# A recurrent attention and a maxout network on one core: another order of all engines' work

## The chip, the core and the metric

The kernel runs on one core of a Trainium2 chip. The core has TensorE (PE), VectorE (DVE), ScalarE (ACT), GpSimd (POOL) and a queue, SyncE (SP), from which the kernel issues nearly all of its DMAs. The metric is device microseconds of one execution. The kernel before takes 147.53 us, the median of 3 runs (147.34 to 148.29).

## The reference

Two parts, one behind the other. The first is a recurrent attention with a decay for each row of its state, over 4 batches, 8 heads, 768 tokens and a head size of 48:

```python
for t in range(S):
    state = alpha[:, :, t, :, None] * state + np.einsum('bhd,bhe->bhde', k[:, :, t], v[:, :, t])
    y[:, :, t] = np.einsum('bhd,bhde->bhe', q[:, :, t], state)
```

The heads of a token are then put side by side, which gives x with 3072 rows of 384, and a feed-forward network with three gates follows (w1, w2, w3 are 384x768, w_out is 768x384):

```python
h = np.maximum(np.maximum(x @ w1, x @ w2), x @ w3)
return h @ w_out
```

All inputs and the output are float32; the kernel works in float16 with sums in float32.

## The kernel before

The 3072 tokens are cut into 12 **steps** of 256 tokens: step s is chunk s // 4 of batch s % 4. A step has two units (x = 0 and 1) of 128 tokens, and the state of a batch goes from unit to unit. What is done for a step is cut into **pieces**, each a small function that issues one or a few instructions. Nothing plans their order: it is a text, `ORDER` (line 507), of 824 pieces such as `G6@1`, and `emit` (line 501) calls them one after the other. The letter names the piece, the number is its index, the number behind @ the step, and a letter between them chooses the engine where there is a choice: v for DVE, a for ACT, p for GpSimd. Each engine works strictly in the order in which its own pieces stand in that text, and waits where an operand, or a buffer that it is to write, is not ready.

The pieces, by the line that shows in the profile:

- **l, K** load an input (l0 alpha, l1 k, l2 q, l3 v; line 100) or a part of a weight (K0 to K8 of the gates, line 111; K9 to K11 of w_out, line 114), 384 KB each, from SP's queue. Inputs go into rings of 4 buffers, weights into 8 staging buffers. **W** casts a weight part to float16 (GpSimd if no letter is given).
- **H** (line 489) is a warm-up matmul on zeroed data; its result is not used. There are 35.
- **m, N, r, u, w** prepare the decays: m multiplies pairs of alphas (line 192), N and r are logs and inverses on ACT (lines 197 to 208), u and w multiply k and q by them (lines 212 and 216). **c** sums the logs with PE into a PSUM bank `lps`; **f, e, g** are exponentials of it on ACT (lines 244 and 255).
- **k, q** scale k and q by the exponentials (line 261, products of two 128x384 SBUF tiles into `qk`). **V** scales v into `vt`, **v** copies it by units into `vu`.
- **T** transposes `qk` with PE into `tps`, and **t** copies that to `qkT` (128x1024); from step 5 on **D** does both as a DMA transpose from SP's queue (line 304).
- **A** (line 318) computes scores into two banks `aps`, each for half of the heads; **a** (line 327) multiplies each of four banks of a step by the causal mask, always on DVE, into `lat`.
- **S** (line 411) sums k times v into `sps`; **s** adds the kept state to it, **M** and **z** multiply by the decay, **y** casts the result into `st` for the next unit.
- **Y** (line 341) computes y from the scores (Y0, Y2) and from the state (Y1, Y3) into `yps`; **x** casts it to `xT`.
- **G** (line 442) is one of nine gate products of a step: `Gi` with i = 3 jg + g is gate g for a third jg of the 768 columns; six 128x256 matmuls into a bank `gps`. It needs the weight part of the same number. **h** takes it out of PSUM: a cast where g = 0 (on ACT unless a letter says otherwise), a maximum with the one before on DVE where g is 1 or 2 (line 459). **O** (line 475) multiplies by w_out, and **o** scales the result (line 164 or 166) and issues the store (line 484).

All PSUM tiles share one ring of 8 banks (`bank`, line 181), handed out in the order of the text, so a PE piece can wait for an `h`, `a`, `s` or `t` that has yet to read an old bank. SP has at most 8 of its DMAs under way: each waits for the one eight places earlier, and a DMA that waits for its data holds all behind it.

```python
for piece in order.split():
    piece, _, step = piece.partition("@")
    i = piece[1:].rstrip("vpa")
    pieces[piece[0]](int(step), int(i), piece[1 + len(i):])
```

Of the kernel before, what the change touches and what calls it, by code (L numbers as in the profile page):

```python
# [25 lines left out]
def kernel(  # L26
# [474 lines left out]
    def emit(order):  # L501
# [16 lines left out]
        G3@0 G3@1 Y0@2 Y3@2 h3a@1 W5p@0 h4v@1 s1v@2 m0v@4 G5@1 x0a@2 h3a@0 G5@0 x1a@2 N0@4 k1v@3 G1@2 G0@2
        G3@2 c0@4 G4@2 h5v@1 h4v@0 w0p@3 K8@0 q1p@3 h0a@2 h3a@2 T1@3 G5@2 u0p@3 h5v@0 h4v@2 q0p@3 k0p@3
        T0@3 W6a@0 f0@4 e0@4 t0a@3 g0@4 V0p@3 t1v@3 h1v@2 h5v@2 m0v@5 G6@1 G6@0 A0@3 A1@3 S0@3 h6a@1 r0@4  # L520
        s0a@3 N0@5 M1p@0 W7p@0 a3@3 h6v@0 a1@3 G2@2 G6@2 G7@1 G7@0 z0p@3 a0@3 h2v@2 a2@3 c0@5 y0a@3 W8a@0
        G8@2 G8@0 l2@4 K10@0 u0p@4 k0p@4 z1p@0 q1p@4 k1p@4 h7v@0 s1v@3 h8v@0 r1@4 y1a@0 l3@4 Y3@3 Y0@3
        x0v@3 G8@1 h7v@1 h8v@1 G7@2 h6a@2 W10a@0 w0p@4 x1a@3 V0a@4 T1@4 G3@3 K11@0 q0p@4 T0@4 e0@5 t1a@4
        h7v@2 h8v@2 l1@5 t0v@4 G7@3 G0@3 u0p@5 K9@0 f0@5 h3a@3 g0@5 h0a@3 l0@6 l3@5 v0p@4 A0@4 l2@5 l0@7
        S0@4 A1@4 W9a@0 W11a@0 k0v@5 M0v@5 a1@4 m0v@6 l0@8 l1@6 l2@6 s0v@4 N0@6 v1a@4 r0@5 M0v@4 M1p@1
        z1p@1 z0p@4 V0p@5 k1p@5 q1p@5 a0@4 a3@4 G1@3 G6@3 G5@3 l3@6 O1@2 h1v@3 a2@4 o1v@2 s1v@4 c0@6 m0p@7
        f0@6 h6a@3 O0@2 G2@3 h7v@3 h2v@3 g0@6 e0@6 r1@5 y0a@4 G4@3 S0@5 Y1@4 Y2@4 Y3@4 Y0@4 O0@1 D1@5 r0@6
        x1a@4 x0a@4 N0@7 r1@6 r0@8 w0v@5 q0p@5 h4v@3 h5v@3 s0v@5 q1p@6 u0p@6 D0@5 G0@4 l1@7 l2@7 z0v@5
        G3@4 c0@7 w0p@6 q0p@6 s1v@5 h0v@4 k1v@6 o0v@2 k0p@6 y1p@1 h3v@4 G4@4 O0@0 G8@3 G1@4 D0@6 D1@6
        h8v@3 h1v@4 G7@4 O1@1 f0@7 v1a@5 l1@8 l0@9 h4v@4 l2@8 r1@8 e0@7 r0@7 g0@7 l3@7 V0a@6 o0a@1 v0v@5  # L530
        A0@5 A1@5 a1@5 a3@5 M1p@3 m0p@8 o0a@0 N0@8 a2@5 a0@5 M0v@6 O1@0 G6@4 c0@8 h6a@4 G2@4 g0@8 o1a@0
        y0p@5 u0v@7 r1@7 h2v@4 o1v@1 M1p@2 z1p@2 v1p@6 k1p@7 Y1@5 Y0@5 w0p@7 x0v@5 q0p@7 Y3@5 Y2@5 h7v@4
        e0@8 x1a@5 f0@8 G8@4 G5@4 G6@5 v0p@6 h5v@4 M0p@8 q1p@7 G7@5 G3@5 h8v@4 h6a@5 S0@6 A1@6 A0@6 h7v@5
        k0v@7 s0v@6 a3@6 a0@6 a1@6 D1@7 D0@7 l0@10 l1@9 l2@9 O0@4 z0p@6 a2@6 M0p@7 y1p@2 y0v@6 s1v@6 M1v@4
        O1@4 G8@5 G0@5 Y3@6 Y1@6 Y0@6 x0v@6 o0v@4 h8v@5 Y2@6 x1v@6 u0v@8 h3a@5 z1p@4 k1p@8 m0p@9 k0p@8
        w0p@8 q0p@8 h0a@5 G1@5 O0@3 G4@5 G2@5 G5@5 D0@8 q1v@8 h4v@5 D1@8 l3@8 N0@9 V0a@7 h1v@5 h5v@5 G3@6
        G4@6 v1a@7 h3a@6 h2v@5 h4v@6 G6@6 o0a@3 h6a@6 A0@7 A1@7 S0@7 a2@7 v0p@7 z1p@3 a1@7 o1v@4 s0v@7
        r0@9 r1@9 O1@5 z0p@7 u0p@9 G0@6 G2@6 c0@9 a0@7 h0a@6 l2@10 l3@9 l0@11 s1v@7 m0v@10 a3@7 G5@6 G1@6
        G7@6 O0@5 r0@10 y1a@3 h1v@6 h5v@6 y0v@7 h7v@6 O1@3 l1@10 G8@6 e0@9 o0a@5 r1@10 o1a@3 f0@9 g0@9
        Y1@7 Y0@7 w0p@9 h2v@6 V0v@8 x0a@7 Y3@7 Y2@7 x1a@7 N0@10 A0@8 S0@8 A1@8 G6@7 s0v@8 c0@10 f0@10  # L540
        h8v@6 a3@8 q0p@9 M1p@5 z1p@5 k0p@9 v0p@8 y1p@4 D0@9 h6a@7 a0@8 a2@8 G8@7 o1a@5 k1v@9 q1v@9 z0v@8
        G1@7 G3@7 v1p@8 D1@9 h3a@7 y1a@5 V0a@9 y0a@8 G4@7 h4v@7 a1@8 G0@7 O1@6 m0p@11 G5@7 Y0@8 Y2@8 Y1@8
        Y3@8 h0v@7 h5v@7 h1v@7 x0v@8 N0@11 g0@10 o1a@6 x1a@8 G7@7 c0@11 e0@10 f0@11 w0p@10 u0p@10 M1p@6
        G2@7 G0@8 G3@8 h7v@7 h8v@7 h2v@7 M0v@9 G1@8 e0@11 r0@11 g0@11 O0@7 A1@9 v0a@9 h0a@8 h3v@8 k1v@10
        S0@9 A0@9 h1v@8 M1v@7 z1v@6 k0p@10 q0p@10 q1p@10 s0v@9 r1@11 l2@11 G4@8 G6@8 a2@9 z0p@9 w0v@11
        a1@9 G7@8 O1@7 G5@8 M0p@10 q1p@11 M0p@11 l3@10 l1@11 y0p@9 D1@10 D0@10 V0p@10 v1a@9 y1a@6 h6a@8
        G8@8 h7v@8 a0@9 a3@9 h8v@8 O0@6 o1a@7 o0a@7 G2@8 h4v@8 o0v@6 k1p@11 h2v@8 h5v@8 Y3@9 Y1@9 Y0@9
        Y2@9 x0a@9 x1a@9 A1@10 A0@10 S0@10 a3@10 D1@11 l3@11 V0a@11 a2@10 a1@10 G4@9 G6@9 u0p@11 q0p@11
        G3@9 G1@9 G5@9 k0v@11 s0v@10 h3v@9 h4v@9 G8@9 G7@9 h5v@9 D0@11 O1@8 h6v@9 a0@10 h7v@9 G0@9 v0p@10
        z0p@10 y0p@10 v1p@10 h8v@9 Y0@10 Y1@10 x0v@10 Y3@10 Y2@10 z1p@7 y1v@7 h0a@9 x1a@10 S0@11 A0@11  # L550
        A1@11 s0v@11 o1v@8 a0@11 z0v@11 a1@11 a3@11 h1v@9 a2@11 v1p@11 y0p@11 v0a@11 G2@9 O0@8 G3@10 G0@10
        G7@10 G4@10 h2v@9 Y3@11 Y0@11 Y2@11 Y1@11 h3v@10 h0a@10 x0a@11 h4v@10 x1v@11 G5@10 G6@10 G1@10
# [40 lines left out]
```

## Time and profile before

| | us |
|---|---|
| median of 3 runs | 147.53 |
| the profiled execution | 146.9 |
| its span | 145.1 |
| 648 matmuls of the gates (line 442), busy | 77.9 |
| 150 matmuls of the output projection (line 475), busy | 26.6 |
| 35 warm-up matmuls (line 489), busy | 11.7 |
| 48 masks on DVE (line 327), busy | 30.7 |
| 72 maxima on DVE (line 459), busy | 48.6 |

The page gives one profiled execution. The granted TensorE clock is 1.0 throughout. DMA moves 250 to 350 GB/s up to about 53 us, and little after 120 us. Busy time alone does not tell what bounds the kernel: the chain of waits and the timeline do, and the prediction shows their lines.

### The profile page before, as it was taken

How to read it: one execution, taken by the hardware profiler on the slowest of the kernel's cores; microseconds unless marked ns; L12 is line 12 of the kernel's file. 1: busy time of each engine (PE TensorE's matmuls, PEld its weight loads, DVE VectorE, ACT ScalarE, POOL GpSimd, SP SyncE). 2: the span in 40 equal slices, each digit the busy share in tenths (PEclk: the TensorE clock that was granted, in tenths of full speed). 3: DMA queues.
4: the chain of work that ended last, by engine and by line, in shares of the span. 5: the costliest groups of instructions: out<-in, count | busy, mean ns of one | idle time of the engine just before them, and what ended most of it. 6: DMA issues, size and time to landing. Idle time of an engine off the chain costs nothing.

```text
span 145.1 us, 5795 instructions
## 1 busy us (share of the span) xinstructions
PE 138.5 (95%) x2450; PEld 107.0 (74%) x2450; DVE 124.6 (86%) x238; ACT 86.0 (59%) x178; POOL 94.4 (65%) x139
## 2 busy tenths in 40 slices
...
GB/s 118 321 325 325 354 249 339 299 268 300 273 335 332 271 290 299 156 220 208 290 330 171 249 204 250 330 298 186 262 215 148 133 179 19 44 0 113 0 81 190
...
## 3 DMA queue, kind: packets, MB, share of 16 engines
...
q8 instruction: 19, 0.31, 0.9%
q10 hardware_dynamic: 288, 0.20, 0.8%
...
## 4 chain that ended last, share of the span: by engine, by line
PE 87%; DVE 7%; ACT 2%; issue 1%; ACTq 0%; DVEq 0%
PE gps L442 46%; PE ops L475 16%; PE yps L341 7%; PE wps L489 6%; PE aps L318 4%; PE sps L411 2%; DVE lat L327 2%; PE tps L296 2%; DVE qk L261 1%; PE lps L223 1%; DVE qkT L160 1%; DVE pa L192 1%; PE lps L235 1%; DVE h L459 1%; ACT h L158 1%
## 5 line engine op out<-in xcount | busy, mean ns | idle before, releaser
L442 PE MATMUL gps<-xT,wcat 128*128 128x256 f16 x648 | 77.9, 273 | 0.0
L442 PEld LDWEIGHTS <-wcat 128*128 128x128 f16 x648 | 61.3, 98 | 9.9
L327 DVE TENSOR_TENSOR lat<-aps,cp 128x512 f16<-128x512 f32 x48 | 30.7, 679 | 0.7 <-PE aps L318 0.6
L158 ACT CAST h<-gps 128x512 f16<-128x512 f32 x27 | 15.8, 586 | 20.0 <-PE gps L442 15.5
L459 DVE TENSOR_TENSOR hT<-gps,h 128x512 f16<-128x512 f32 x36 | 24.2, 684 | 2.9 <-PE gps L442 2.2
L475 PE MATMUL ops<-wo,hT 128*128 128x384 f16 (+1 forms) x150 | 26.6, 320 | 0.0
L459 DVE TENSOR_TENSOR h<-gps,h 128x512 f16<-128x512 f32 x36 | 24.4, 682 | 1.4 <-ACT h L158 0.8
L475 PEld LDWEIGHTS <-hT 128*128 128x128 f16 x150 | 14.1, 98 | 7.3
L164 ACT ACTIVATE ob<-ops,c 128x384 f32<-128x384 f32 (+1 forms) x16 | 8.5, 560 | 8.6 <-PE ops L475 8.6
L489 PE MATMUL wps<-wo 128*128 128x512 f16 x35 | 11.7, 459 | 1.2 <-DVE wo L560 1.2
L426 POOL TENSOR_TENSOR kept<-full,gm 128x192 f32<-128x192 f32 x15 | 7.6, 506 | 7.8 <-DVE full L421 3.6
L261 POOL TENSOR_TENSOR qk<-rq,ac 128x384 f16<-128x384 f32 x10 | 10.0, 1008 | 4.0 <-ACT ac L244 4.0
L261 POOL TENSOR_TENSOR qk<-qa,ac 128x384 f16<-128x384 f32 x9 | 9.4, 1040 | 3.4 <-ACT ac L244 3.0
L158 ACT CAST xT<-yps 128x384 f16<-128x384 f32 x16 | 7.3, 481 | 6.1 <-PE yps L341 5.8
L160 POOL COPY vu<-vt 64x384 f16<-64x384 f16 x18 | 9.7, 536 | 1.8 <-issue 1.2
L164 ACT ACTIVATE vt<-rv,c 128x768 f16<-128x768 f32 x7 | 6.5, 933 | 6.8 <-DMA rv<-in_v_dram 6.7
L318 PE MATMUL aps<-qkT 48*64 48x128 f16 x384 | 8.7, 219 | 0.6 <-DVE qkT L160 0.5
L160 POOL CAST wcat<-ws 128x768 f16<-128x768 f32 x6 | 5.3, 888 | 5.9 <-DMA ws<-in_moe_w_dram 5.9
L160 POOL CAST st<-kept 64x192 f16<-64x192 f32 x18 | 6.7, 370 | 3.0 <-DVE kept L426 2.2
L318 PEld LDWEIGHTS <-qkT 48*64 48x64 f16 x384 | 6.1, 106 | 3.2 <-issue 1.3
L160 DVE CAST h<-gps 128x512 f16<-128x512 f32 x9 | 6.1, 680 | 2.2 <-PE gps L442 2.2
L261 POOL TENSOR_TENSOR qk<-rk,ic 128x384 f16<-128x384 f32 x7 | 7.6, 1090 | 0.1
...
## 6 DMA issues: line engine op xcount, KB each, us to landing
...
qkT<-qk SPq DMA_TRANSPOSE x14, 4.1
```

Source lines behind the costliest of these rows:

```text
L158: nc.scalar.copy(out=dst, in_=src)
L160: engines[eng].tensor_copy(out=dst, in_=src)
L164: nc.scalar.mul(dst, src, col)
L261: engines[eng or "p"].tensor_mul(dst.rearrange("p a b c -> p (a b) c")[:, :, :D], near_of.pop((s, n)) if r == 0 and s not in FINE else raw ...
L318: nc.tensor.matmul(aps[i][half * J:(half + 1) * J, col, :], qkT[rows, r, 1, p, cols], qkT[rows, :, 0, p, cols], start=True, stop=True)
L327: nc.vector.tensor_mul(*(t.rearrange("p a t -> p (a t)").rearrange("p (a n) -> p a n", n=n) for t in (lat_of[s, u][:, i], aps_of[s, u][i]) ...
L341: nc.tensor.matmul(y_of[s, x][C * m:C * (m + 1), f, :], lhs, rhs, start=(s, x, m) not in begun, stop=last[x] and n == len(todo) - 1)
L426: engines[eng or "p"].tensor_mul(kept, full_of.pop((s, x)), gm_of.pop((s, x)).unsqueeze(2).broadcast_to([P, HP, D]))
L442: nc.tensor.matmul(gps[:, j, :], wcat[:, f, g, jj * P:(jj + 1) * P], xT[:, f].rearrange("p u t -> p (u t)"), start=(f == 0), stop=(f == NF ...
L459: nc.vector.tensor_max(h, gps, h_of[s, i - 1])
L475: nc.tensor.matmul(ops_of[s, o], hT_of[s][:, jj, u * P:(u + 1) * P], wo16[:, jj, cols], start=(jj == 0), stop=(jj == NJ - 1))
L489: nc.tensor.matmul(wps, blank[:, :P], blank, start=True, stop=True)
```

## The change

Only the text of `ORDER` changes. Both texts hold the same 824 pieces with the same indices and steps; what differs is where they stand and, for some, which engine they name. Pieces by engine, where the numbers differ (no letter counted as the piece's default):

| piece | before | after |
|---|---|---|
| q scale | 19 GpSimd, 5 DVE | 12 GpSimd, 12 DVE |
| k scale | 13 GpSimd, 11 DVE | 14 GpSimd, 10 DVE |
| V values | 3 GpSimd, 7 ACT, 2 DVE | 8 ACT, 4 DVE |
| v unit copies | 9 GpSimd, 6 ACT, 1 DVE | 5 GpSimd, 10 ACT, 1 DVE |
| W weight casts | 6 GpSimd, 6 ACT | 2 GpSimd, 10 ACT |
| u, w | 7 GpSimd, 2 DVE each | 5 GpSimd, 4 DVE each |
| m pair decays | 5 GpSimd, 4 DVE | 4 GpSimd, 5 DVE |
| M gate products | 13 GpSimd, 7 DVE | 10 GpSimd, 10 DVE |
| t qkT copies | 6 DVE, 4 ACT | 5 DVE, 5 ACT |
| h casts (g = 0) | 27 ACT, 9 DVE | 30 ACT, 6 DVE |
| y state spreads | 9 GpSimd, 7 ACT, 4 DVE | 12 GpSimd, 5 ACT, 3 DVE |
| s | 3 ACT, 17 DVE | 2 ACT, 18 DVE |

The beginning and the end of the text:

```diff
     ORDER = """
-        H1@0 l0@0 H1@0 H1@0 H1@0 H1@0 H1@0 H1@0 H1@0 H1@0 l0@1 H1@0 H1@0 H1@0 H1@0 H1@0 N0@0 c0@0 N0@1
-        l2@0 l1@0 l2@1 H1@0 c0@1 H1@0 H1@0 H1@0 H1@0 H1@0 H1@0 f0@0 q0v@0 f1@0 l1@1 l3@0 e0@0 l3@1 l0@2
-        l0@3 e1@0 q1p@0 K0@0 g0@0 f1@1 k1p@0 k0v@0 f0@1 g0@1 T0@0 t0v@0 M0v@1 K1@0 l2@2 H1@0 l1@2 K2@0
-        H1@0 T1@0 e1@1 H1@0 H1@0 H1@0 l3@2 e0@1 K4@0 q0p@1 V0a@0 K3@0 t1v@0 A1@0 H1@0 K5@0 q1p@1 k0p@1
-        M0p@0 k1v@1 A0@0 S0@0 s0a@0 z0p@0 y0p@0 m0p@3 H1@0 T1@1 T0@1 H1@0 l2@3 l0@4 a3@0 a2@0 a0@0 a1@0
-        V0a@1 W0p@0 t0a@1 S0@1 H1@0 H1@0 H1@0 Y3@0 l1@3 N0@2 t1v@1 Y0@0 s1v@0 s0v@1 z0v@1 s1v@1 x1v@0
-        x0a@0 K6@0 N0@3 A1@1 A0@1 a3@1 l3@3 l0@5 H1@0 c0@2 H1@0 a1@1 a0@1 H1@0 a2@1 K7@0 g0@2 c0@3 f1@2
-        e1@2 y0v@1 G0@0 Y0@1 W1p@0 W2p@0 f0@2 Y3@1 q0v@2 q1v@2 e0@2 k0v@2 k1v@2 x0a@1 x1a@1 h0a@0 G1@0
-        G1@1 T0@2 f0@3 g0@3 e0@3 t0a@2 h1v@0 W4p@0 M0p@2 T1@2 G0@1 G2@0 t1v@2 V0v@2 r0@3 h0a@1 A1@2 A0@2
...
-        h5v@11 h7v@11 h8v@11 O2@11 o1v@9 o1a@10 O3@11 o0v@11 O4@11 O5@11 o1a@11 O6@11 o2a@11
+        H1@0 H1@0 H1@0 H1@0 H1@0 H1@0 H1@0 H1@0 H1@0 H1@0 l0@0 N0@0 l0@1 H1@0 H1@0 H1@0 H1@0 N0@1 l2@0
+        c0@0 f0@0 q0v@0 e0@0 f1@0 l1@0 k0v@0 l3@0 e1@0 H1@0 H1@0 c0@1 H1@0 H1@0 l1@1 l2@1 k1v@0 q1v@0
+        V0v@0 l3@1 H1@0 H1@0 H1@0 T0@0 l0@2 f1@1 e0@1 g0@1 e1@1 g0@0 t0a@0 l0@3 K0@0 H1@0 T1@0 k1p@1 k0v@1
+        M0v@0 q1v@1 t1a@0 H1@0 S0@0 H1@0 K1@0 l2@2 l1@2 K2@0 H1@0 H1@0 H1@0 A0@0 A1@0 f0@1 q0p@1 s0a@0
+        l3@2 V0a@1 T1@1 z0p@0 y0p@0 K4@0 H1@0 H1@0 T0@1 H1@0 W0p@0 M0p@1 a2@0 a3@0 a1@0 t1a@1 t0v@1 S0@1
+        H1@0 Y3@0 A0@1 a0@0 s1v@0 H1@0 K3@0 N0@2 H1@0 H1@0 Y0@0 A1@1 a1@1 s0v@1 z0p@1 c0@2 m0v@3 x0v@0
+        x1a@0 r0@3 N0@3 y0p@1 f0@2 f1@2 W1a@0 H1@0 c0@3 a2@1 a0@1 a3@1 G0@0 Y0@1 Y3@1 h0v@0 G1@0 e1@2 e0@2
+        K5@0 x1a@1 x0v@1 q1p@2 s1v@1 k1v@2 k0v@2 r1@3 e0@3 f0@3 g0@2 q0v@2 W2a@0 G0@1 T1@2 G1@1 T0@2 l0@4
+        G2@0 h0a@1 g0@3 t0a@2 t1v@2 h1v@0 V0v@2 h1v@1 h2v@0 G2@1 W4a@0 W3a@0 S0@2 A0@2 A1@2 M0p@2 s0v@2
+        a1@2 a3@2 l1@3 G4@1 G4@0 h2v@1 z0p@2 a0@2 a2@2 G3@1 G3@0 m0v@4 y0p@2 W5a@0 h3a@1 G5@1 Y3@2 Y0@2
+        h4v@1 x0v@2 h3a@0 G5@0 h4v@0 h5v@0 N0@4 c0@4 x1a@2 g0@4 l2@3 q1v@3 M0v@4 w0v@3 G3@2 h3v@2 s1v@2
+        G5@2 G4@2 h4v@2 h5v@1 u0p@3 k1p@3 q0p@3 k0p@3 h5v@2 K6@0 l3@3 T1@3 G0@2 l1@4 f0@4 W6a@0 h0a@2
+        t1a@3 r0@4 V0a@3 e0@4 G1@2 h1v@2 l0@5 G2@2 K7@0 T0@3 G6@0 G6@1 S0@3 t0v@3 h2v@2 l2@4 h6a@0 W7a@0
+        A0@3 u0p@4 m0v@5 K8@0 A1@3 a1@3 N0@5 s0a@3 a0@3 q1v@4 G6@2 l3@4 k1p@4 M1p@0 M0p@3 z0p@3 y0p@3 G7@1
...
+        G4@11 G5@11 G7@11 G8@11 h4v@11 h5v@11 h6v@11 O0@10 G1@11 G2@11 O1@10 O1@9 h7v@11 o0v@10 h8v@11
+        o1a@9 o1a@10 h1v@11 h2v@11 O2@11 O3@11 o0v@11 O4@11 O5@11 o1a@11 O6@11 o2v@11
     """
```

In SP's queue the first 19 DMAs are the same in both, with one pair of input loads (l2@1 and l3@0) swapped among them; K6 stays at place 23, K7 goes from place 26 to 27 and K8 from 28 to 29.

More of the change, by code (lines that the diff above doesn't have):

```diff
@@ L513 @@
-        V0a@1 W0p@0 t0a@1 S0@1 H1@0 H1@0 H1@0 Y3@0 l1@3 N0@2 t1v@1 Y0@0 s1v@0 s0v@1 z0v@1 s1v@1 x1v@0
-        x0a@0 K6@0 N0@3 A1@1 A0@1 a3@1 l3@3 l0@5 H1@0 c0@2 H1@0 a1@1 a0@1 H1@0 a2@1 K7@0 g0@2 c0@3 f1@2
-        e1@2 y0v@1 G0@0 Y0@1 W1p@0 W2p@0 f0@2 Y3@1 q0v@2 q1v@2 e0@2 k0v@2 k1v@2 x0a@1 x1a@1 h0a@0 G1@0
-        G1@1 T0@2 f0@3 g0@3 e0@3 t0a@2 h1v@0 W4p@0 M0p@2 T1@2 G0@1 G2@0 t1v@2 V0v@2 r0@3 h0a@1 A1@2 A0@2
-        S0@2 h2v@0 G2@1 s0a@2 l1@4 r1@3 z0p@2 y0p@2 M0p@3 a3@2 W3a@0 G4@1 G4@0 a0@2 a2@2 a1@2 h1v@1 h2v@1
@@ L518 @@
[L518 to L552, printed above, removed]
@@ L553 @@
-        h5v@10 h1v@10 G4@11 O0@9 G1@11 G0@11 G5@11 o0a@9 o0a@8 h6a@10 h0v@11 h1v@11 O1@9 G2@10 G2@11
-        h2v@11 h7v@10 G8@10 G3@11 h3a@11 h2v@10 h8v@10 h4v@11 G8@11 G6@11 G7@11 O0@10 h6a@11 O1@10 o0a@10
-        h5v@11 h7v@11 h8v@11 O2@11 o1v@9 o1a@10 O3@11 o0v@11 O4@11 O5@11 o1a@11 O6@11 o2a@11
+        H1@0 H1@0 H1@0 H1@0 H1@0 H1@0 H1@0 H1@0 H1@0 H1@0 l0@0 N0@0 l0@1 H1@0 H1@0 H1@0 H1@0 N0@1 l2@0
+        c0@0 f0@0 q0v@0 e0@0 f1@0 l1@0 k0v@0 l3@0 e1@0 H1@0 H1@0 c0@1 H1@0 H1@0 l1@1 l2@1 k1v@0 q1v@0
@@ new lines @@
+        t1a@3 r0@4 V0a@3 e0@4 G1@2 h1v@2 l0@5 G2@2 K7@0 T0@3 G6@0 G6@1 S0@3 t0v@3 h2v@2 l2@4 h6a@0 W7a@0
+        A0@3 u0p@4 m0v@5 K8@0 A1@3 a1@3 N0@5 s0a@3 a0@3 q1v@4 G6@2 l3@4 k1p@4 M1p@0 M0p@3 z0p@3 y0p@3 G7@1
+        r1@4 h6a@1 G7@0 K10@0 l0@7 W8a@0 a3@3 T1@4 a2@3 c0@5 h7v@0 h7v@1 G7@2 G8@1 f0@5 h6a@2 w0p@4 l1@5
+        h8v@1 g0@5 Y3@3 M1v@1 Y0@3 x0a@3 e0@5 x1a@3 s1v@3 t1v@4 G8@2 q0p@4 k0p@4 K11@0 K9@0 G8@0 T0@4 G1@3
+        G0@3 G6@3 z1p@0 h8v@0 z1v@1 h7v@2 h8v@2 G3@3 V0a@4 r0@5 W10a@0 h0a@3 r1@5 h6a@3 t0v@4 h1v@3 A1@4
@@ new lines @@
+        a2@4 l2@5 l0@6 l3@5 y1p@0 v0p@4 m0p@7 S0@4 A0@4 s0v@4 a0@4 G5@3 G4@3 G2@3 k1v@5 h3a@3 W9a@0 W11p@0
+        u0p@5 l1@6 l2@6 l0@8 l0@9 z0p@4 l1@7 k0p@5 O1@2 O0@2 v1a@4 y0a@4 V0a@5 h4v@3 a3@4 s1v@4 a1@4 o0a@2
+        h2v@3 m0v@6 Y2@4 Y0@4 Y3@4 Y1@4 S0@5 M0p@5 w0p@5 N0@6 x1a@4 x0a@4 G8@3 G7@3 q0p@5 q1p@5 h5v@3
+        s0v@5 z0v@5 h7v@3 c0@6 D1@5 r0@6 e0@6 f0@6 g0@6 r1@6 G0@4 O0@1 D0@5 h8v@3 k1v@6 u0v@6 q1v@6 k0p@6
+        N0@7 o0a@1 h0a@4 G6@4 O1@1 c0@7 G7@4 G8@4 G3@4 h6a@4 m0v@9 M1v@2 h7v@4 G5@4 G4@4 w0v@6 D1@6 l2@7
@@ new lines @@
+        l3@6 f0@7 y1a@1 r0@7 z1p@2 q0p@6 h3a@4 h8v@4 o1v@2 y0v@5 D0@6 l3@7 l1@8 l3@8 l1@9 l2@8 l0@10 o1a@1
+        A0@5 g0@7 e0@7 A1@5 a0@5 a1@5 r0@8 v1a@5 v0a@5 a3@5 a2@5 O0@0 G1@4 y1p@2 G2@4 Y1@5 h1v@4 k1v@7
+        Y0@5 M1p@3 m0p@8 u0v@7 s1v@5 h2v@4 h4v@4 h5v@4 V0v@6 Y3@5 Y2@5 x0a@5 x1a@5 O1@0 G6@5 G3@5 G4@5
+        r1@7 O0@4 o1a@0 h6a@5 h3a@5 M0v@6 A0@6 S0@6 h4v@5 o0v@4 A1@6 v0p@6 w0p@7 a1@6 s0v@6 N0@9 N0@8
+        z0p@6 o0a@0 v1a@6 y0p@6 a0@6 G7@5 a3@6 G5@5 k0p@7 q1p@7 h5v@5 h7v@5 s1v@6 a2@6 q0v@7 G2@5 O1@4
@@ new lines @@
+        c0@9 V0a@8 c0@8 G0@5 g0@8 v0a@8 Y2@6 Y0@6 Y1@6 x0a@6 f0@8 r1@8 Y3@6 D1@7 D0@7 M0v@8 u0v@8 x1v@6
+        G8@5 G1@5 e0@8 h0a@5 q1v@8 h8v@5 G5@6 o1v@4 M1p@4 w0v@8 z1p@3 h1v@5 k0p@8 V0v@7 k1p@8 q0p@8 h2v@5
+        D0@8 z1p@4 D1@8 G3@6 G0@6 G4@6 G1@6 h3a@6 r0@9 r0@10 r1@9 G2@6 O0@3 h0a@6 f0@9 e0@9 v1a@8 h4v@6
+        g0@9 o0a@3 m0p@10 v0p@7 u0p@9 y1p@3 h5v@6 M0v@7 h1v@6 l2@9 l3@9 l0@11 l2@10 l1@10 G6@6 G7@6 h2v@6
+        h6a@6 S0@8 s0v@8 v1p@7 S0@7 A1@7 A0@7 z0p@8 h7v@6 a2@7 k1p@9 O1@5 G8@6 O1@3 a0@7 O0@5 M0v@9 a3@7
@@ new lines @@
+        s0v@7 h8v@6 a1@7 z0v@7 o1a@3 y0a@7 N0@10 y0p@8 y1p@4 M1p@5 s1v@7 A0@8 A1@8 Y0@7 Y1@7 Y2@7 Y3@7
+        a0@8 O0@6 k0v@9 x0v@7 x1a@7 o0a@6 o1a@5 a2@8 w0v@9 G8@7 G6@7 h6a@7 q0p@9 G7@7 m0p@11 N0@11 r0@11
+        a3@8 a1@8 q1v@9 D0@9 D1@9 h7v@7 o0a@5 Y1@8 Y3@8 Y0@8 Y2@8 c0@10 G4@7 G0@7 G1@7 x1v@8 x0v@8 G0@8
+        G1@8 f0@10 h8v@7 l3@10 h0v@7 g0@10 h0a@8 e0@10 V0a@9 q1v@10 G3@7 G2@8 u0p@10 c0@11 h1v@8 M1p@6
+        z1p@5 h3a@7 M0p@10 h1v@7 h2v@8 k1p@10 r1@10 g0@11 e0@11 w0p@10 z1p@6 G6@8 G5@7 h4v@7 h6a@8 r1@11
```

9 lines of the change are left out of this document (added).

## Prediction

> **What bounds the kernel now.** I read the page's busy times first, then the chain of waits, then the timeline of the first 43 us and the busy times by stage. In the page (engine, busy us, share of the span, instructions):
>
> ```profile
> PE 138.5 (95%) x2450; PEld 107.0 (74%) x2450; DVE 124.6 (86%) x238; ACT 86.0 (59%) x178; POOL 94.4 (65%) x139
> ```
>
> The chain (start, us, engine, tile, line, instructions) shows where those 138.5 us of PE are needed work and where they fill time:
>
> ```profile
> 1.17 5.50 PE wps L489 x14
> ...
> 13.00 2.40 DVE lat L327 x4
> ...
> 20.65 0.68 PE gps L442 x6
> ...
> 39.80 0.65 PE aps L318 x32
> 40.45 0.26 PE sps L411 x31
> 40.71 2.73 PE gps L442 x24
> ...
> 137.73 3.77 PE ops L475 x28
> ```
>
> From 39.80 to 141.50 every piece of the chain is PE with none waiting: there no order can be faster. Before that the chain goes through DVE and ACT. The 35 warm-up matmuls (wps) all stand ahead of the first gate product G0@0, which the timeline starts at 20.51. So an order can win only in two places: when G0@0 starts, and what PE loses between G0@0 and about 42. Three rows of PE idle in that stretch, two weight casts that gate it, and the load that one of them waits for (start, duration, engine, operation, idle before it):
>
> ```profile
> 20.51 0.81 PE L442 MATMUL gps<-xT,wcat 128*128 128x256 f16 x6
> ...
> 21.98 0.42 PE L341 MATMUL yps<-lat,vt 64*32 64x128 f16 x32 [0.31 <-issue]
> ...
> 27.63 0.34 PE L411 MATMUL sps<-vt,qk 64*64 64x48 f16 x20 [0.28 <-issue]
> ...
> 31.77 1.81 SPq L111 DMA_DIRECT2D ws<-in_moe_w_dram  x1
> ...
> 33.74 1.32 POOL L261 TENSOR_TENSOR qk<-qa,ac 128x384 f16<-128x384 f32 x1
> ...
> 34.12 1.35 DVE L261 TENSOR_TENSOR qk<-rk,ic 128x384 f16<-128x384 f32 x1
> ...
> 40.33 0.82 POOL L160 CAST wcat<-ws 128x768 f16<-128x768 f32 x1
> ```
>
> **The parts: who does what.** No piece is added or removed; 824 stand in both orders. By the engine letters GpSimd loses 7 q products, 4 weight casts, 3 value scalings, 4 unit copies, 2 near-k, 2 near-q, 1 pair decay and 3 gate products, and gains a k product and 3 state spreads. With its rows (1.03, 0.89, 2.20, 2 x 0.54, 1.00, 1.09, 1.07, 0.28; 1.09, 2 x 0.37 us) that is -7.2 -3.6 -6.6 -4.3 -2.0 -2.2 -1.1 -0.8 +1.1 +2.2 = -24.5 us: 94.4 falls to about 70. ACT gets 4 casts, 1 value scaling, 3 h casts, a qkT copy (1.01) and 4 unit copies, and gives 2 spreads and a state copy: +3.3 +0.9 +1.8 +1.0 +4.1 -1.4 -0.3 = +9.4, to 95. Neither is near the bound: no sum needs more of them than that their products come in time. DVE gets 7 q products, 2 value scalings, 2 near-k, 2 near-q, 1 pair decay, 1 state copy, 3 gate products and gives 3 h casts, a qkT copy, a k product and a spread: 7 x 0.58 + 2 x 0.61 + 4 x 0.55 + 0.55 + 0.34 + 0.3 - 2.0 - 0.7 - 0.85 - 0.6 = about +4.5, to 129 us. That one is near the bound. Counted along DVE's queue up to the pair decay of step 5 (39.8 in the trace), 8 of the 12 extra pieces are before it; behind it the queue has 6 h pieces, 2 xT and a k fewer, and 5 q, 2 u, a w, a V, a qkT copy and three small ones more: -3.6 -0.9 -0.5 +2.3 +0.9 +0.5 +0.5 +0.6 +0.5 = +0.3 at their pace undisturbed, and I take +0.9, since products between SBUF tiles are also lengthened (rival B).
>
> **The start, up to G0@0.** The first load (l0@0) and its order of issue stay, and 14 warm-ups still stand ahead of c0@0, so c0@0 is at 6.67 as before. Then the orders part. Both qkT copies of step 0 move from DVE (0.68, at 10.36 and 11.57) to ACT, where they follow the exponentials of both steps: at 0.37 to 0.50 us each these end at 10.75, the copies take to 12.7, and f0@1 and s0a@0, whose PSUM banks the scores of step 0 need, to 13.45. The masks of step 0 so start at 13.75, against 12.92: 0.8 us later. DVE meanwhile does V0@0, k1@0 and q1@0, which filled ACT and GpSimd. From there: masks at 0.60 each with t0@1 between, to 16.75; A0@1 waits for the last of them for its bank; three warm-ups (0.66) and Y0@0 (0.70) end at 18.45; x0 and x1 of step 0 are there at 19.0. In before Y0@0 ended at 18.22 and xT at 18.86. W0p@0 ends at 19.21 in both, its load is the 11th in both. G0@0 then waits for c0@3, whose logs follow m0v@3, x1a@0 and r0@3: 19.8, so c0@3 is done at 20.1 and G0@0 starts there. Against 20.51 that is 0.4 us early; I take 0.3 either way as its error.
>
> **G0@0 to G7@1.** Between these two the same pieces stand in both orders, only shuffled: 21 gates at 0.655 (13.8 us), 2 x 0.95 for Y, 4 x 0.45 for T, 4 x 0.29 for A, 2 x 0.35 for S, 0.24 for c0@4: 19.6 us. Before takes from 20.51 to 42.04 (third gate from 40.71), so it loses 1.9 us. In the new order I walk the waits: G0@1 waits 0.3 for x1a@1 (22.5); G2@0 0.1 for W2a@0; G4@1 0.1 for W4a@0, since ACT has t0a@2 ahead of it; the banks of G2@2 (s1v@2), G6@1 (h5v@1) and A0@3 (t0v@3, 38.0) come free just in time by DVE's sums, and A0@3 is at 38.4, against 39.80. G6@2 ends at 39.65. Then G7@1 needs W7a@0, and the load for it has moved from 26th to 27th in SP's queue (l1@4 is ahead of it now; l0@4, l1@3 and l2@3 ahead of K6 are the same three in another order). It was issued at 31.77 and took at most 6.8 us (that is the longest of these loads), so it landed at 38.6; a load of 384 KB at the 325 GB/s of the page takes 1.2 us, so it lands at 39.8, the cast ends at 40.6, and so begins G7@1: PE idles 0.9 us, and is still **1.45 us ahead** of 42.04. The fewer loads ahead of the first gate are so only in the text's order: the first 19 loads that SP issues are the same.
>
> **Behind G7@1** PE's work is the same again, 99.5 us without a gap, so it ends 1.45 us earlier if the others keep pace. K8 is one place later too (about 42.1, its cast 42.9), and G8@1 comes at 43.3. In SP's queue the transpose D0@6 now stands behind the store o1@2, which waits for a late scaling on DVE (after h8@4); the scores that need it come 7.6 us of PE pieces later, and a transpose lands 4.1 us after its issue, so it is hidden unless DVE is 3 us late. DVE:
>
> ```profile
> 40.00:60.00 20.00, 19.13 (x37) 1.00 1.03 291
> ...
> sum 80.00, DVE 76.06; mean DVE 19.02
> ```
>
> From 40 to 120 DVE is idle 3.9 us of 80 (second column busy us). The added 0.9 fits in; locally it may not: around G2@7, x0v@9 and G1@9 DVE has 7.4 us of h, z and x to do between two PE pieces that are 7.15 apart. I charge 0.2 us (none to 1.0). **At the end** the last store's scaling goes from ACT to DVE beside ACT's: of the 0.73 us of two such on ACT 0.3 would go, but SP's issues are 0.4 apart behind one another; 0.1 us. O2@11 needs h2v@11: when G2@11 ends, DVE still has h1v@11 and h2v@11 to do, 1.4 us; the two projections now placed there (1.94) hide it, and without them it would cost that 1.4.
>
> **The sum**: -1.45 + 0.2 - 0.1 = -1.35 us. The profiled execution was 146.9 (span 145.1, so 1.8 around it); the median 147.53 is 0.6 above it. So 143.75 us of span, and **146.2 us** for the median.
>
> **Rivals.** *A, nothing left.* The lead is eaten by what it runs into. For: the gates of K7 and K8 come from loads that are later, and in the timeline SP's issues stood for up to 2.9 us (25.34); one such stop ahead of K7 costs 0.8 more, and the DVE stretch its 1.0. Against: most loads are 1.2 us apart wherever I can see them. -1.45 + 0.8 + 1.0 - 0.1 = +0.25: 147.8; with one of the two alone, 147.0.
>
> *B, DVE becomes the bound, slower.* Products with two SBUF inputs stretch on DVE when GpSimd works:
>
> ```profile
> L261 DVE TENSOR_TENSOR qk<-rk,ic x8: 545/823/1349, 8.8 to 103.9; 128x384 f16<-128x384 f32 x8
> ```
>
> Alone 0.55, at worst 1.35 (min, median, max in ns), and in the two rows at 33.74 and 34.12 both sides are longer at once: GpSimd's 1.32 against 1.00. Behind step 5's pair decay there were 14 such products on DVE, now 21; their mean stretch from 40 to 125 was 0.12. At a mean of 0.40 the 21 cost 5.9 more, with the 0.9 that is 6.8; less the idle 3.9 it is 2.9 late, less the 1.35 gained: +1.55, 149.1; with the products bunched at steps 6 to 9 (q, u, w, V), where the idle time elsewhere does not help, up to 150. DVE becomes the bound from a mean of 0.26 (21 x 0.14 + 0.9 uses up the 3.9), and eats the lead at 0.33. Against it: GpSimd is busy 70 us, not 94, so fewer of them can meet it.
>
> The Trainium skill (SBUF — State Buffer, "Who interferes with whom") says that a DVE instruction with two SBUF inputs and a GpSimd instruction that reads SBUF lock each other out for a whole instruction. By that rule, if meetings fall at random, a product waits half of GpSimd's 1.0 us with a chance of 70/145, an estimate of 0.24 each: short of what decides, so the sum would stay at 146.2. The trace agrees in part: the DVE row ends 0.41 behind the GpSimd row that it met, not 0.55.
>
> **From these to the numbers.** Forecast 0.52, own range 145.2 (K7 not late: 0.9 more) to 147.0 (start error and DVE's 1.0 against me). A 0.24, B 0.24. Low 145.2, high 149.5, which leaves out the worse third of B and the edges. About 1% (1.5 us) is what one can tell from no change: faster is below 146.05, slower above 149.0. Faster: 0.32 of the forecast and 0.01 of A, 0.33. Within: 0.20, 0.23 of A and 0.02 of B, 0.45. Slower: 0.22.
>
> **What would show it.** G0@0 (first gps row) near 20.1; the masks of step 0 at 13.7; A0@3 near 38.4; a PE wait for ACT's wcat cast ahead of G7@1 near 40.6; then no PE idle and DVE below 97% from 40 to 120. It is wrong if G0@0 is later than 20.5, if PE waits for DVE in the middle, or if DVE's q products are above 0.8 us in the mean.

## The result, and the profile after

The changed kernel took **148.63 us** (median of 20 executions, 147.06 to 151.81), beside 147.39 for the kernel before in the same series (20 executions, 145.88 to 149.59): a ratio of 1.0085 with a 95% interval of 1.0061 to 1.0109. It is 1.24 us slower by the medians, less than the 1% that the prediction set as its bound; 146.2 had been forecast.

A later series ran both again: 148.71 against 147.38. Another ran the kernel before against itself and gave 0.990 (0.984 to 0.996; 147.17 against 147.76 by the medians), so such an interval is too narrow by itself. Below, times are medians of all executions of one series, and a wait counts only where a trace shows it.

The engines do what the change says. Busy time in the page of after (148.34 us, span 146.5):

```profile
PE 139.7 (95%) x2450; PEld 107.5 (73%) x2450; DVE 127.6 (87%) x249; ACT 94.4 (64%) x190; POOL 71.0 (48%) x116
```

In the kernel before, the chain of waits was PE alone from 39.80 on. In after the view of the chain begins at 107.86, on DVE, and is PE alone only from 114.50 on (start, us, what):

```profile
112.71 1.27 DVE qk L261
113.98 0.48 DVE xT L160
114.46 0.05 issue
114.50 2.14 PE gps L442 x18
...
139.11 3.93 PE ops L475 x30
```

The 1.27 us product is k0@11, and x0@9, which G1@9 needs, stands behind it in DVE's queue. The timeline of DVE, GpSimd and PE there:

```profile
112.56 1.00 POOL L261 TENSOR_TENSOR qk<-rq,ac 128x384 f16<-128x384 f32 x1
...
112.63 1.35 DVE L261 TENSOR_TENSOR qk<-ka,ic 128x384 f16<-128x384 f32 x1
...
113.51 1.32 POOL L216 TENSOR_TENSOR qa<-rq,ra 128x384 f32<-128x384 f32 x1
113.90 0.54 DVE L160 CAST xT<-yps 128x384 f16<-128x384 f32 x1
...
114.50 2.14 PE L442 MATMUL gps<-xT,wcat 128*128 128x256 f16 x18 [0.70 <-DVE xT L160]
```

DVE's product begins 0.07 behind GpSimd's q1@11 and takes 1.35 instead of 0.55; PE stands 0.70 us. A second wait lies ahead of G7@1, where the prediction had put one, but with another cause:

```profile
40.31 1.00 POOL L261 TENSOR_TENSOR qk<-rk,ic 128x384 f16<-128x384 f32 x1 [1.34 <-ACT ic L244]
...
40.34 0.84 PE L318 MATMUL aps<-qkT 48*64 48x128 f16 x32
40.35 1.38 DVE L192 TENSOR_TENSOR pa<-ra 128x384 f32<-128x384 f32 x1
40.58 0.86 ACT L158 CAST wcat<-ws 128x768 f16<-128x768 f32 x1
...
41.65 1.27 DVE L327 TENSOR_TENSOR lat<-aps,cp 128x512 f16<-128x512 f32 x2
...
42.38 1.36 PE L442 MATMUL gps<-xT,wcat 128*128 128x256 f16 x11 [0.44 <-DVE lat L327]
```

W7a@0 (the ACT cast) is done at 41.44. What comes last is the mask a1@3 (41.65, the first of two), which frees the bank that G7@1 writes. It stands behind the pair decay m0@5, which again meets a GpSimd product and takes 1.38. The stages behind it (stretch, its length, then busy us and instructions of PE, PEld, DVE, ACT and GpSimd, granted clock, share of the DMA engines, GB/s):

```profile
40.00:60.00 20.00, 19.56 (x437) 15.91 (x436) 19.09 (x34) 16.82 (x35) 16.16 (x23) 1.00 1.00 284
60.00:80.00 20.00, 20.00 (x351) 15.41 (x350) 19.21 (x39) 15.92 (x36) 10.95 (x17) 1.00 1.06 262
80.00:100.00 20.00, 20.00 (x361) 15.79 (x360) 19.49 (x36) 12.89 (x30) 14.76 (x25) 1.00 0.97 214
100.00:120.00 20.00, 19.30 (x295) 15.54 (x293) 18.93 (x37) 12.27 (x25) 9.46 (x14) 1.00 0.92 192
```

DVE is idle 3.3 us of 80 (3.9 before): it is not full as a whole, and PE idles only where one of the two waits is. Where the time went, from two profiles of each kernel (starts and ends of pieces in the traces):

| us | before | before, again | after | after, again |
|---|---|---|---|---|
| first sums c0@0 start | 6.50 | 6.53 | 7.01 | 6.52 |
| G0@0 starts | 20.51 | 20.25 | 21.05 | 20.46 |
| G7@1 starts | 41.96 | 42.53 | 42.38 | 42.90 |
| last matmul ends | 141.65 | 142.39 | 143.03 | 143.57 |
| from G7@1 to there | 99.69 | 99.86 | 100.65 | 100.67 |

In the mean 0.39 us are lost up to G7@1 and 0.88 behind it: 1.27 together, close to the 1.24 of the medians. The first is no larger than what two profiles of one kernel differ by there; the second is clear of that. Of the 1.45 us of lead that had been forecast nothing is to be seen.

### The profile page after: what moved, and what is told of

The parts are those of the page before. It is cut to its first block, busy times and chain, and to the rows that moved or that the text cites. A ratio compares the mean times of both kernels' runs of the same rounds, so it can differ in the third digit from the quotient of the medians.

```text
span 146.5 us, 5799 instructions
## 1 busy us (share of the span) xinstructions
PE 139.7 (95%) x2450; PEld 107.5 (73%) x2450; DVE 127.6 (87%) x249; ACT 94.4 (64%) x190; POOL 71.0 (48%) x116
## 5 line engine op out<-in xcount | busy, mean ns | idle before, releaser
L442 PE MATMUL gps<-xT,wcat 128*128 128x256 f16 x648 | 76.9, 273 | 1.1 <-DVE xT L160 0.7
L158 ACT CAST h<-gps 128x512 f16<-128x512 f32 x30 | 17.4, 589 | 12.2 <-PE gps L442 8.8
L475 PEld LDWEIGHTS <-hT 128*128 128x128 f16 x150 | 14.2, 98 | 7.6
L261 POOL TENSOR_TENSOR qk<-qa,ac 128x384 f16<-128x384 f32 x7 | 7.3, 1044 | 6.6 <-DVE qa L216 6.5
L318 PE MATMUL aps<-qkT 48*64 48x128 f16 x384 | 9.6, 220 | 0.9 <-DVE lat L327 0.4
L158 ACT COPY vu<-vt 64x384 f16<-64x384 f16 x20 | 10.2, 509 | 0.3
L261 DVE TENSOR_TENSOR qk<-rq,ac 128x384 f16<-128x384 f32 x10 | 6.4, 644 | 4.0 <-ACT ac L244 4.0
L261 POOL TENSOR_TENSOR qk<-ka,ic 128x384 f16<-128x384 f32 x7 | 7.5, 1071 | 4.6 <-DVE ka L212 3.2
L160 POOL CAST st<-kept 64x192 f16<-64x192 f32 x24 | 8.5, 354 | 1.2
L160 POOL COPY vu<-vt 64x384 f16<-64x384 f16 x10 | 5.1, 510 | 6.2 <-DVE gm L398 5.4
L164 ACT ACTIVATE vt<-rv,c 128x768 f16<-128x768 f32 x8 | 7.5, 937 | 0.2
```

What stands on the lines that cost most here:

```text
L158: nc.scalar.copy(out=dst, in_=src)
L160: engines[eng].tensor_copy(out=dst, in_=src)
L164: nc.scalar.mul(dst, src, col)
L261: engines[eng or "p"].tensor_mul(dst.rearrange("p a b c -> p (a b) c")[:, :, :D], near_of.pop((s, n)) if r == 0 and s not in FINE else raw ...
L318: nc.tensor.matmul(aps[i][half * J:(half + 1) * J, col, :], qkT[rows, r, 1, p, cols], qkT[rows, :, 0, p, cols], start=True, stop=True)
L442: nc.tensor.matmul(gps[:, j, :], wcat[:, f, g, jj * P:(jj + 1) * P], xT[:, f].rearrange("p u t -> p (u t)"), start=(f == 0), stop=(f == NF ...
```

## The experiments

No run leaves out work that the output needs.

**Which half is slow?** Two hybrids are cut behind G7@1, each with the pieces that remain in the other kernel's order. At the cuts they differ from the new and from the old order by:

```diff
-        M0p@3 z0p@3 y0p@3 G7@1 r1@4 h6a@1 G7@0 K10@0 l0@7 W8a@0
+        M0p@3 z0p@3 y0p@3 G7@1 h6a@1 a3@3 G7@0 a2@3 c0@5 W8a@0
...
-        G2@2 G6@2 G7@1 G7@0 z0p@3 a0@3 h2v@2 a2@3
+        G2@2 G6@2 G7@1 M0v@4 h2v@2 l2@4 u0p@4 a0@3
```

> The new order up to and including G7@1, then the remaining pieces in the old order with the old engine letters. Theory 1 (two local waits: G7@1 behind a mask that follows a stretched pair decay, and G1@9 behind x0@9 that follows a stretched k product; the first warm-ups differ by chance of the execution): no wait of PE near G1@9, G7@1 within 0.4 of before's, so 0.0 to +0.4 us against the kernel before. Theory 2 (the new start itself is late by 0.5 whenever it runs): +0.4 to +0.6. Theory 3 (DVE is short of time over the whole middle, because of the extra products): the old rest has none of them, so -0.1 to +0.2, with no more PE waits than before's.

> The old order up to and including G7@1, then the remaining pieces in the new order with the new engine letters. Theory 1 (two local waits): PE waits about 0.7 once, near G1@9 for x0@9, and nowhere else behind 42 us: +0.7 to +0.9 us against the kernel before. Theory 2 (the new start is late by itself): the old start has no such lateness, so at most +0.8, all of it from G1@9. Theory 3 (DVE is short over the whole middle): PE waits in several places, +1.2 or more.

Measured: 150.44 and 150.15 us, before 147.66. The first is far above what any theory gave for it. The second lies within theory 3's "+1.2 or more", but not for its reason: PE waits in two places behind 42 us, ahead of G1@9 and at the seam, which makes a wait of its own. There, with the old start and the new rest, T1@4 waits for a product that the old start had not got ready:

```profile
44.71 0.54 DVE L261 TENSOR_TENSOR qk<-rq,ac 128x384 f16<-128x384 f32 x1
...
45.31 0.62 PE L296 MATMUL tps<-cp,qk 128*128 128x128 f16 x8 [1.38 <-DVE qk L261]
```

What can be taken from them: the new rest waits 0.69 us ahead of G1@9 behind the old start too, and the old rest does not wait there (it has its own 0.70 ahead of G6@5 instead, for x of step 5). The halves can't be priced in this way.

**The wait at G1@9.** First k0@11 behind x1@9, and then, in a run of its own, about 2 us earlier, which leaves DVE the same work ahead of x0@9:

```diff
-        o1v@7 Y1@9 V0a@10 v1a@10 o1a@6 k0v@11 Y2@9 Y0@9 Y3@9 x0v@9 x1a@9 A0@10
+        o1v@7 Y1@9 V0a@10 v1a@10 o1a@6 Y2@9 Y0@9 Y3@9 x0v@9 x1a@9 k0v@11 A0@10
...
-        a0@9 u0v@11 M1v@7 z1p@7
+        a0@9 u0v@11 k0v@11 M1v@7 z1p@7
```

> The new order with one piece moved: DVE's k0@11 stands behind x1@9 instead of ahead of x0@9. Theory 1 (local wait): the 0.7 us of PE idle ahead of G1@9 go away and nothing takes their place, so 0.5 to 0.8 us faster than the changed kernel, +0.4 to +0.7 against the kernel before. Theory 3 (DVE is short as a whole): the product only delays the masks and sums of step 10 instead, PE waits there, and the gain is below 0.2: +1.0 to +1.3 against the kernel before.

> The new order with DVE's k0@11 behind u0@11, about 2.5 us earlier than now and still ahead of x0@9, at a time when GpSimd has nothing to do. DVE's work ahead of x0@9 is the same. Theory 1 (the product is stretched because it meets GpSimd's q1@11): 0.55 to 0.70 for it and no PE wait ahead of G1@9, 0.6 to 0.8 us faster than the changed kernel. Rival (DVE simply has too much to do ahead of x0@9): the wait stays at 0.5 or more, and the gain is below 0.2.

> The changed kernel itself once more, for a second profile and beside the runs of this call. Theory 1 (a stretched k0@11 ahead of x0@9): PE waits 0.6 to 0.8 ahead of G1@9 again, 0.4 ahead of G7@1 again; the first sums c0@0 start anywhere from 5.6 to 7.0 with the moment at which the warm-ups turn from 0.43 to 0.21, and G0@0 14.0 to 14.2 behind them; PE's own stall inside Y0@1 is again at its matmul number 350 and anything from 0 to 1.3 long. Median +0.8 to +1.3 us against the kernel before. Rival (all of this was luck of one profile): no wait ahead of G1@9.

Measured: 147.89 with k0@11 behind (before 147.66). In one series the changed kernel took 148.71 (again 0.70 of wait at G1@9 and 0.44 at G7@1), and k0@11 earlier 148.02: 0.69 less. The timeline of the earlier one:

```profile
110.42 0.56 DVE L261 TENSOR_TENSOR qk<-ka,ic 128x384 f16<-128x384 f32 x1
...
113.49 0.55 DVE L160 CAST xT<-yps 128x384 f16<-128x384 f32 x1
...
114.09 0.61 PE L442 MATMUL gps<-xT,wcat 128*128 128x256 f16 x4
```

With GpSimd waiting, the same product takes 0.56, and PE does not stand. The medians alone would not settle it, for the twelve executions of each overlap (147.59 to 149.64 and 147.11 to 148.94). The traces do: from G7@1 to the end of the last matmul the three profiles with k0@11 in its place take 100.65 to 100.69 us, the three with it moved and nothing else changed behind G7@1 99.89 to 99.99. So it is the meeting that costs, not the amount of DVE's work, and 0.7 us of the 1.24 to 1.33 lost are settled.

**The wait at G7@1.** It was taken away in two ways: m0@5 behind the masks (with k0@11 behind x1@9), and m0@5 on GpSimd, alone and with k0@11 earlier.

```diff
-        A0@3 u0p@4 m0v@5 K8@0 A1@3 a1@3 N0@5 s0a@3 a0@3 q1v@4
+        A0@3 u0p@4 K8@0 A1@3 a1@3 s0a@3 a0@3 m0v@5 N0@5 q1v@4
...
-        A0@3 u0p@4 m0v@5 K8@0
+        A0@3 u0p@4 m0p@5 K8@0
```

> The new order with two moves: k0@11 behind x1@9 as before, and the pair decay m0@5 (with N0@5 behind it on ScalarE) behind the masks a1@3 and a0@3. Theory 1 (two local waits): G7@1 no longer waits for the mask a1@3 (0.4 gained, up to 0.8 with the idle time around A1@3) and G1@9 no longer for x0@9 (0.7): -0.1 to +0.3 us against the kernel before, the rest being the start. Theory 2 (the new start is late by itself): not under +0.3. Theory 3 (DVE is short as a whole): +0.8 or more.

> The new order with one letter changed: the pair decay m0@5, which DVE does ahead of the mask a1@3, is done by GpSimd, in a stretch where GpSimd waits 1.3 us for an exponential. Theory 1 (the bank of G7@1 comes free late because the stretched m0@5 stands ahead of a1@3): no PE wait ahead of G7@1, 0.6 to 0.8 us gained there, and as nothing is put in DVE's queue in its place the gain holds to the end: 147.9 to 148.2. Rival (DVE is the bound from 42 on): the gain at G7@1 is given back at T1@4, c0@5 or later, as it was when m0@5 was moved behind the masks, and the time is that of the changed kernel, 148.6.

> The new order with both repairs: m0@5 on GpSimd and k0@11 behind u0@11. Theory 1: neither wait, 0.7 + 0.7 less than the changed kernel: 147.2 to 147.5, level with or below the kernel before. Rival (DVE is the bound from 42 on): 147.9 to 148.1, as with k0@11 alone.

Measured: 148.26 (before 147.66), 148.84 and 148.46 (before 147.57). The wait at G7@1 is gone in all three traces, and no time is gained: with k0@11 repaired as well they are no faster than with k0@11 alone. From A0@3 to G7@1 each takes 1.44 us instead of the 2.04 of all profiles of the new order that keep m0@5 in place, so the repair is worth 0.60 there. In the last of them PE is 1.41 us ahead of the run with k0@11 earlier at 65 us (the other 0.81 come from an earlier start and shorter stalls of this execution), 0.73 at 75 and 0.13 behind at 100. Two of its waits of PE (line, waited for: us, times, longest):

```profile
PE aps L318 <- DMA qkT<-qk: 0.9, 2, 0.7
...
PE aps L318 <- DVE st L160: 0.3, 1, 0.3
```

The scores of steps 6 and 7 wait for qkT, which DMA transposes write, those of step 5 for the state that DVE casts (`st`). The lead falls at just these pieces, by 0.34 at A0@5, 0.33 at A0@6 and 0.80 at A1@7. DVE, too, waits there for a load, and PE stands longest at A1@7:

```profile
80.60 0.56 DVE L261 TENSOR_TENSOR qk<-rq,ac 128x384 f16<-128x384 f32 x1 [0.71 <-DMA rq<-in_q_dram]
...
88.18 0.64 PE L318 MATMUL aps<-qkT 48*64 48x128 f16 x32 [0.66 <-DMA qkT<-qk]
```

The DMAs did not become earlier with PE but later. The k load of step 7 landed at 62.61 (60.62 in the run that PE was 1.4 behind), the q load of step 8 at 80.51 (79.60). That is no chance of one execution: in the three runs with m0@5 moved the k load of step 7 landed at 62.61 to 63.42, in the six profiles of the new order with m0@5 in place at 58.90 to 60.66. The two with both repairs end their last matmul even later than the runs with k0@11 alone that they led by 1.42 and 1.26 at G7@1 (142.74 us in both, against 142.62 and 142.11). So it is not only that a lead runs into something that does not move with PE: with m0@5 moved, PE takes 1.5 to 1.9 us more behind G7@1 (101.54 and 101.78, against 99.89 to 99.99), for the 0.60 gained ahead of it.

A last run tried to let the transposes past the loads, by two moves in SP's queue on top of both repairs:

```diff
-        l0@8 l0@9 z0p@4 l1@7 k0p@5
+        l0@8 l0@9 z0p@4 k0p@5
...
-        G0@4 O0@1 D0@5 h8v@3
+        G0@4 O0@1 D0@5 l1@7 h8v@3
...
-        D0@6 l3@7 l1@8 l3@8 l1@9 l2@8 l0@10
+        D0@6 l3@7 l2@8 l1@8 l3@8 l1@9 l0@10
```

> m0@5 on GpSimd and k0@11 behind u0@11 as before, and two loads moved in SP's queue: the k load of step 7 behind the transposes of step 5, and the q load of step 8 ahead of the k load of step 8. Theory D (the lead of 1.4 us at G7@1 is given back at the scores of steps 5, 6 and 7 because the transposes that they read stand behind loads in the DMA queues): the waits ahead of A0@5, A0@6 and A1@7 (1.5 us together in the run without this) shrink to below 0.6, and the time is 147.3 to 147.9. Rival (the DMA engines are busy without a pause there, so moving a load only moves the wait): 148.2 to 148.7, with the same sum of waits in the middle.

Measured: 149.75 us (before 147.76). No wait is left at A0@5, A0@6 or A1@7, but the v load of step 8, now one place later, landed at 80.14 (76.98 without the two moves), ACT's scaling of it stood ahead of x0@6, and PE waited for that (timeline of ACT and PE):

```profile
80.16 0.94 ACT L164 ACTIVATE vt<-rv,c 128x768 f16<-128x768 f32 x1 [4.82 <-DMA rv<-in_v_dram]
...
82.20 0.48 ACT L158 CAST xT<-yps 128x384 f16<-128x384 f32 x1
...
82.73 1.47 PE L442 MATMUL gps<-xT,wcat 128*128 128x256 f16 x12 [2.05 <-ACT xT L158]
```

Neither theory had said so. The transposes of step 5 did land earlier (62.51 and 63.69, against 64.07 and 64.97 without the two moves), those of step 6 did not (67.73 and 73.63, against 66.81 and 73.19), and PE itself was about 1.3 us later in this execution at 45 us, which alone can take such waits away. So theory D is not shown; what is shown is that with these two moves a load came 3.2 us later and PE waited 2.05 us for it. Why the loads land later when m0@5 is moved stays open.

**The start.** Three warm-ups fewer ahead of c0@0, alone and with k0@11 behind x1@9, and the kernel before once more:

```diff
-        H1@0 l0@0 N0@0 l0@1 H1@0 H1@0 H1@0 H1@0 N0@1 l2@0
+        H1@0 l0@0 N0@0 l0@1 H1@0 N0@1 l2@0
```

> The new order with 11 warm-ups instead of 14 ahead of c0@0 (32 in all). Theory W (c0@0 is held by warm-ups at 0.43 each where they turn fast late, not by its logs, which end at 6.13): c0@0 starts at 6.0 to 6.4 in such an execution, and the whole kernel is 0.4 to 0.6 faster then, 0.2 to 0.5 in the median. Rival (the warm-ups are needed: with a gap ahead of c0@0 PE stays slow for longer): the real matmuls of the start run at half speed and the kernel is 0.5 us or more slower.

> The new order with k0@11 behind x1@9 and 11 warm-ups instead of 14 ahead of c0@0. If both theories hold their gains add, since nothing in between waits for a load: 0.7 + 0.3 = 1.0 us faster than the changed kernel, 147.2 to 147.6, level with the kernel before. If DVE is the bound behind G7@1, an earlier start is given back between 42 and 110, and it is no faster than with k0@11 moved alone.

> The kernel before once more, for a second profile of it. If the start of the first profile was typical, G0@0 is at 20.5 and G7@1 near 42.0 again. If the first profile was an early one (its own time was 0.6 below the median), G7@1 is at 42.3 to 42.7, by longer stalls of PE at its matmuls 222, 350 or 478, and the new order's start then gains nothing and loses nothing against it. Behind G7@1 99.6 to 99.8 us to the last matmul's end, with no wait of PE over 0.2, in either case.

Measured: 148.78 and 148.02 in the series of the changed kernel's 148.71, so nothing is gained by fewer warm-ups, and 147.17 for the kernel before against its own 147.76. c0@0 did start earlier, at 5.86 in both, though its first matmuls then took 0.32 instead of 0.16 (four of them, and one in the second run), and G0@0 at 20.44 and 20.05; yet G7@1 came at 43.14 and 42.99, later than in any run with 14. PE's timeline of the first of them shows where (idle time in brackets):

```profile
22.13 0.41 PE L341 MATMUL yps<-lat,vt 64*32 64x128 f16 x29 [0.45 <-issue]
...
27.30 0.33 PE L318 MATMUL aps<-qkT 48*64 48x128 f16 x9
...
28.87 0.53 PE L318 MATMUL aps<-qkT 48*64 48x128 f16 x23 [1.25 <-issue]
```

PE stands in the middle of a piece, for nothing that a semaphore shows. The kernel before has the same stalls, in other pieces; in its second profile:

```profile
26.84 0.26 PE L411 MATMUL sps<-vt,qk 64*64 64x48 f16 x12
...
28.20 0.34 PE L411 MATMUL sps<-vt,qk 64*64 64x48 f16 x20 [1.09 <-issue]
```

Counted from the first matmul, these stalls stand at matmul 350 and at matmul 478 (from 0) in both kernels and in every order tried. With three warm-ups fewer each wait for a semaphore moved three matmuls down, from 755 to 752 and from 2074 to 2071; these two stayed. In the old order PE also stands at matmul 222, ahead of G0@0 (0.46 and 0.19 in the two profiles of before), again 128 matmuls earlier. 128 matmuls with their weight loads are 256 instructions. The DMA view from 26 to 27 us of the same run (packets, MB, share of 16 engines) has one packet that is not the kernel's data:

```profile
q8 instruction: 1, 0.02, 7.0%
```

That queue moves 19 packets with 0.31 MB in the whole span, 16 KB each. This one moved from 26.26 to 27.37, and PE went on at 28.87, 1.5 us behind it. At every stall of 0.17 us or more at these two places, in all profiles of this study, such a packet ended 1.3 to 1.7 us ahead of PE's restart. I read it so: up to about 29 us PE can be no earlier than its next block of instructions, which comes through the same 16 DMA engines as the loads; no run took loads away to test that. The stall at 350 was 0 to 1.22 us and that at 478 0 to 1.29 us.

## Why the prediction was wrong, point by point

In the prediction's own sum, -1.45 + 0.2 - 0.1, it is the first term that failed most. After reaches G7@1 not 1.45 us earlier than before but 0.39 later, the 0.2 charged to DVE behind it became 0.88, and the end gave nothing. The step under the first term is the loss of 1.9 us between G0@0 and G7@1 that a better order was to win back: more than half of it was work. That stretch, first in before, then in after (its length, then busy us and instructions of PE, and the others as above):

```profile
20.51:41.96 21.45, 20.60 (x449) 17.16 (x446) 19.61 (x33) 15.07 (x33) 14.12 (x18) 1.00 1.03 302
...
21.05:42.38 21.33, 20.56 (x446) 17.12 (x443) 20.58 (x38) 16.84 (x33) 9.55 (x14) 1.00 1.08 323
```

- **Who does what: right.** GpSimd was to fall to about 70, ACT to rise to 95, DVE to 129; they are at 71.0, 94.4 and 127.6.
- **The start: first half right, second half 0.3 to 0.4 us too short.** The prediction's 6.67 for c0@0 is where its row of warm-ups ends; the first sums of before begin at 6.50. Counted from there the masks of step 0 were forecast 7.25 us behind c0@0, and in both profiles of after they begin 7.26 behind it. But from the masks to G0@0 6.35 us were forecast, and 6.68 to 6.78 are taken in all profiles with the new start and 14 warm-ups; A0@1's wait for a mask alone is 0.36 in each. So G0@0 follows c0@0 by 13.9 to 14.2 us, and the old start needs 13.5 to 14.0: the new one gains nothing. The error of 0.3 that was allowed also left out that c0@0 itself comes anywhere from 5.67 to 7.01.
- **"19.6 us" of work from G0@0 to G7@1: too small by 0.9 to 1.0. This is the step that failed.** In this stretch PE is busy for 20.60 us in before and 20.56 in after (20.49 in its second profile). So of the 1.9 us that the old order "loses", 1.0 was work, and 0.6 of the rest, 0.31 and 0.28, was the stalls at matmuls 350 and 478, and 0.2 a wait at A0@3. The prediction quoted both stalls as rows of PE idle that an order could win back; they come and go between executions of one order. Its walk also left out its own waits: 38.4 for A0@3 is G0@0 at 20.1 and 18.3 us of work, without the 0.5 that it names on the way. The three profiles read for this have 18.9 to 19.1 there, stalls for instructions left out.
- **The wait at G7@1: place right, cause wrong.** Not K7 and the cast W7a@0 (38.90 and 41.44), but a bank behind a mask behind a stretched pair decay. This is the part of the walk that counted DVE's queue at its undisturbed pace. What the wait costs in the end stays open: the three runs without it gain 0.60 up to G7@1 and lose more behind it.
- **"Behind G7@1 PE's work is the same, so it ends 1.45 us earlier if the others keep pace": DVE did not keep pace at G1@9, and a lead of 1.45 was not tried, since there was none.** Where PE was 1.4 us earlier at 65 us, the transposes and loads were later, and nothing of it was left at 90; but there m0@5 had been moved. Between two executions that differ only in the three warm-ups, both with k0@11 behind x1@9, G7@1 came 0.77 us apart (42.22 and 42.99) and the last matmul ended 0.78 apart (142.11 and 142.89). So a lead of that size is kept; whether 1.45 would have been is open.
- **The DVE stretch at x0@9 and G1@9: right in place, mis-sized.** It was charged with 0.2 (none to 1.0); the product was 0.8 longer, and PE stood 0.70.
- **The end: no gain.** The span ends 3.47 us behind the last matmul in the first profile of before and 3.52 in that of after.
- **Rivals.** A, with DVE late at G1@9, came nearest; its 147.8 is 0.8 too low, since there was no lead to eat. B had the right mechanism and the wrong condition: from 40 to 125 us 22 products with two SBUF inputs were stretched by 0.17 in the mean, short of the 0.26 that it asked for, but four of them were 0.8 longer each, and two of the four stood ahead of what PE waited for next.

The rule of the Trainium skill (SBUF — State Buffer, "Who interferes with whom") was made into 0.24 a product by taking meetings as random. In a fixed order they are not: the same four products meet GpSimd in both profiles of the changed kernel, and each takes 0.78 to 0.83 more. The traces agree with it in part: k0@11 takes 0.56 where GpSimd stood, and in both places above DVE ended 0.42 behind the GpSimd product that it met, not the 0.55 of a whole product. The one that begins first is not lengthened: in after, m0@6 on DVE began at 56.82 and took 0.55, and GpSimd's q1@5, which began 0.01 behind it, took 1.38 instead of 1.00.

What remains open: after the repair of G1@9 the kernel is still 0.2 to 0.6 us slower than before by the medians (147.89 against 147.66, 148.02 against 147.38), of which the profiles put at most 0.3 behind G7@1 (99.89 to 99.99, against 99.69 and 99.86) and the rest ahead of it, where two profiles of one kernel differ by as much. Executions of one kernel spread by more than this, so a difference of this size is not clear of noise. No version tried beats the kernel before.
